# The start of a tuned kernel rearranged: two turns of z in front, casts on another engine, loads in another order

## The chip, the cores and the metric

One core of a Trainium2 chip runs the whole program. The metric is the device time of one execution in microseconds; the median of several executions is quoted. Instruction times come from one profiled execution of each kernel, counted from its first instruction.

## The reference

Eight batches of an attention without softmax, gated by u, then a two-layer network with a sigmoid-approximated GELU over all 24064 tokens:

```python
# u, v: (8, 3008, 256); z: (8, 3008, 64); w_in: (256, 2048); w_out: (2048, 256), all fp32
scores = (1 / S) * matmul(z, z.T)          # S = 3008, per batch
attn   = maximum(scores, 0) ** 2
x      = (u * matmul(attn, v)).reshape(B * S, D)
h      = x @ w_in
out    = (h / (1 + exp(-1.702 * h))) @ w_out
```

## The kernel before

TensorE does everything heavy in fp16. A *scores* step multiplies z by its own transpose into PSUM, ScalarE applies the *relu*, VectorE *squares* it, and TensorE multiplies the square by V (*value matmuls*). For that z must lie transposed in SBUF. In the first batch z is loaded as fp32 in six chunks of up to 512 rows. Each chunk is *cast* to fp16 (two instructions, one for each half of the partitions of the later transpose), *transposed* by TensorE, and *copied* out of PSUM; the three together are called a *turn*. The code counts chunks and turns `g` from 0, this text from 1: turns 3 and 4 are `g` = 2 and 3. V's blocks for the first batch are loaded as fp32 and cast by GpSimd. *Dummy* matmuls on zeros (`keep_warm`) fill idle stretches of TensorE; that they raise its clock or keep it up is what the name intends. TensorE works in the order of the program (before, turns 3 to 6 stand behind 2, 11, 19 and 28 value matmuls, as in the table below), so the tables below decide at which value step a turn, a cast or a scores step stands.

```python
def first_cast(g):                                 # both halves of one chunk's cast, VectorE
    m = g % CB * CB
    for c in range(2):
        dst, src = ZT["st"][g // CB][:, m:m + CB, c, :], ZT["f"][g // CB][:, m:m + CB, :]
        dve.tensor_copy(dst, src)

def first_zt(g):                                   # transposes now, returns the copy for later
    z2 = ZT["st"][g // CB][:, g % CB * CB:(g % CB + 1) * CB]
    if g == 0:
        ...                                        # (cut) turn 1: copied in halves, ScalarE + VectorE
    zp = ZP[g] if g in ZP else ps1.tile([P, CB, P], F16, name="zp", tag="ps1")
    for k in range(CB):
        pe.transpose(zp[:, k, :], z2[:, k, :, :], ident)
    def copies():
        ...                                        # (cut) addresses
        if g > 2:
            act.activation(dst, src, AF.Copy, scale=1.0)
        else:
            dve.tensor_copy(dst, src)
        if nb < CB:
            dve.tensor_copy(zt[:, nb * P:], zp[:, nb, :])
    return copies

def square(b, i, jp, sc):                          # (cut to the first chunk's case)
    rl = pw.tile([P, 2, CH], F16, name="rl", tag="rl", bufs=3)
    act.activation(rl[:, :, :n], sc[:, :, :n], AF.Relu, scale=csc)
    a = pa.tile([P, 2, CH], F16, name="a", tag="a", bufs=26)
    dve.tensor_tensor(a[:, :, :n], rl[:, :, :n], rl[:, :, :n], ALU.mult)

# value step of the first chunk -> turn, cast, number of scores steps
FIRST_ZT, FIRST_CAST = {2: 2, 11: 3, 19: 4, 28: 5}, {2: 3, 8: 4, 16: 5}
SCHED0 = {0: {2: 1, 8: 2, 16: 2, 25: 2, 33: 2, 40: 2}, ...}

# (cut) the start; sp = SyncE's queue, act = ScalarE's
first_z(0, CB, sp)
first_z(CB, 2 * CB, act)
for n0 in (0, VB):
    load_v(0, n0)                # V0: first half on sp, second on act; V1 on sp
first_z(2 * CB, 4 * CB, act)     # z chunks 3 and 4
load_v(0, 2 * VB)
first_z(4 * CB, NJ, sp)          # z chunks 5 and 6
for n0 in range(3 * VB, NJ, VB):
    load_v(0, n0)
keep_warm(7)
for g in range(2):
    first_cast(g)
for copies in [first_zt(g) for g in range(2)]:
    copies()
keep_warm(1)
posts = scores(0, [queue.pop(0) for _ in range(2)])
posts[0]()
first_cast(2)
posts[1]()
keep_warm(3)
posts = scores(0, [queue.pop(0)])
keep_warm(2)
...                          # (cut) PSUM tiles of turns 3 and 4, first load of u
```

The score buffers (`ps2`) are two, the relu buffers three.

Of the kernel before, what the change touches and what calls it, by code (L numbers as in the profile page):

```python
# [15 lines left out]
def kernel(  # L16
# [58 lines left out]
    dve.memset(nil, 0.0)  # L75

    late, LATE = [], []
    ZP = {}
    ZT, V16, UQ, UT, XT, unit, TT = {}, {}, {}, {}, {}, {}, {}

    SYNC = mybir.DependencyInfo(mybir.DependencyClass.Sync, mybir.DependencyReason.DATA)
# [12 lines left out]
    def keep_warm(n):  # L94

        if "w" not in ZT:
            ZT["w"] = ps1.tile([P, CH], F32, name="w", tag="ps1")
        for k in range(n):
            pe.matmul(ZT["w"], nil[:, :P], nil, start=(k == 0), stop=(k == n - 1))  # L99

    def first_z(n0, n1, eng):

        if 0 not in ZT:
            ZT[0] = pz.tile([P, NJ, P], F16, name="ZT", tag="ZT")
            ZT["st"] = [pa.tile([P, CB * CB, 2, DQK], F16, name="zst", tag="tt", bufs=14) for _ in range(2)]
            ZT["f"] = [pw.tile([P, CB * CB, DQK], F32, name="zf", tag="y") for _ in range(2)]
        zf = ZT["f"][n0 // (CB * CB)]
        m0 = n0 % (CB * CB)
        t0, last = n0 * P, n1 == NJ
        t1 = (n1 - CB if last else n1) * P  # L110
        eng.dma_start(
            zf[:, m0:m0 + (t1 - t0) // P, :].rearrange("p (g n) d -> p g (n d)", n=CB),
            z[0, t0:t1].rearrange("(g p n) d -> p g (n d)", p=P, n=CB),
        )
        if last:
            m1 = m0 + (t1 - t0) // P
            eng.dma_start(zf[:, m1:m1 + CB - 1, :], z[0, t1:S0].rearrange("(p n) d -> p n d", n=CB - 1))
            for h in range(2):
                eng.dma_start(zf[h * SREM:(h + 1) * SREM, m1 + CB - 1, :], z[0, S0:S])

    def first_cast(g):
        m = g % CB * CB
        for c in range(2):
            dst, src = ZT["st"][g // CB][:, m:m + CB, c, :], ZT["f"][g // CB][:, m:m + CB, :]
            dve.tensor_copy(dst, src)  # L125

    def first_zt(g):

        z2 = ZT["st"][g // CB][:, g % CB * CB:(g % CB + 1) * CB]
        if g == 0:  # L130
            zh = [ps1.tile([P, CB // 2, P], F16, name="zh", tag="ps1") for _ in range(2)]
            for k in range(CB):
                pe.transpose(zh[k // 2][:, k % 2, :], z2[:, k, :, :], ident)

            def copies():
                dst = ZT[0][:, :CB, :].rearrange("d n p -> d (n p)").rearrange("d (p h n) -> d h p n", h=2, n=CB // 2)
                act.activation(dst[:, 0], zh[0].rearrange("d n p -> d p n"), AF.Copy, scale=1.0)
                dve.tensor_copy(dst[:, 1], zh[1].rearrange("d n p -> d p n"))

            return copies  # L140
        zp = ZP[g] if g in ZP else ps1.tile([P, CB, P], F16, name="zp", tag="ps1")
        for k in range(CB):
            pe.transpose(zp[:, k, :], z2[:, k, :, :], ident)  # L143

        def copies():
            zt = ZT[0][:, g * CB:(g + 1) * CB, :].rearrange("d n p -> d (n p)")
            nb = CB if g < NCH - 1 else CB - 1
            dst = zt[:, :nb * P].rearrange("d (p n) -> d p n", n=nb)
            src = zp[:, :nb, :].rearrange("d n p -> d p n")
            if g > 2:  # L150
                act.activation(dst, src, AF.Copy, scale=1.0)  # L151
            else:
                dve.tensor_copy(dst, src)
# [4 lines that stand above are left out]
# [19 lines left out]
    def load_v(b, n0):  # L177

        if n0 == 0:
            V16[b] = pz.tile([P, NJ, D], F16, name="V16", tag="V16")  # L180
        dst, eng = V16[b][:, n0:n0 + VB], pool
        if b == 0:
            dst, eng = pa.tile([P, VB, D], F32, name="vst", tag="tt", bufs=14), sp
        full = min(VB, NJ - 1 - n0)
        if b == 0 and n0 == 0:
            full = VB // 2
            act.dma_start(dst[:, full:], v[b, full * P:VB * P].rearrange("(n p) c -> p n c", p=P))
        eng.dma_start(dst[:, :full, :], v[b, n0 * P:(n0 + full) * P].rearrange("(n p) c -> p n c", p=P))
        if n0 + VB == NJ:
            for h in range(2):  # L190
                eng.dma_start(dst[h * SREM:(h + 1) * SREM, full, :], v[b, S0:S])
        if b == 0:
            for n in range(0, VB, 2):
                pool.tensor_copy(V16[b][:, n0 + n:n0 + n + 2], dst[:, n:n + 2])
# [380 lines left out]
    def pieces(b, i):  # L575
# [24 lines left out]
    LOADW = {(3, 16): 0, (3, 24): 1, (3, 32): 2, (3, 40): 3, (4, 16): 4, (4, 22): 5, (4, 28): 6, (4, 34): 7}  # L600
    LOAD = {(3, NJ + 20): 4, (4, NJ + 5): 5}

    FIRST_ZT, FIRST_CAST = {2: 2, 11: 3, 19: 4, 28: 5}, {2: 3, 8: 4, 16: 5}
    SCHED0 = {
        0: {2: 1, 8: 2, 16: 2, 25: 2, 33: 2, 40: 2},
        1: {0: 2, 8: 2, 15: 2, 22: 2, 30: 2, 38: 2},
        2: {n: 1 for n in (0, 3, 7, 11, 28, 32, 36, 40, 44)} | {NJ: 2},
        3: {n: 1 for n in (0, 4, 8, 12, 16, 19, 29, 33, 37, 41, 45)} | {NJ: 2},
# [6 lines left out]
    def take(b, n):  # L615
        for post_ in scores(b, [queue.pop(0) for _ in range(n)]):
            post_()
# [7 lines left out]
    first_z(CB, 2 * CB, act)  # L625
    for n0 in (0, VB):
        load_v(0, n0)
    first_z(2 * CB, 4 * CB, act)
    load_v(0, 2 * VB)
    first_z(4 * CB, NJ, sp)  # L630
    for n0 in range(3 * VB, NJ, VB):
        load_v(0, n0)
    keep_warm(7)
    for g in range(2):
        first_cast(g)
    for copies in [first_zt(g) for g in range(2)]:
        copies()
    keep_warm(1)
    posts = scores(0, [queue.pop(0) for _ in range(2)])
    posts[0]()  # L640
    first_cast(2)
    posts[1]()
    keep_warm(3)
    posts = scores(0, [queue.pop(0)])
    keep_warm(2)
    for g in (2, 3):
        ZP[g] = ps1.tile([P, CB, P], F16, name="zp", tag="ps1")
    load_u(0, 1)

    for b in range(B):  # L650
        nup = NCH * NFG
        more = b + 1 < B
        sched = SCHED0 if b == 0 else SCHED if more else SCHED_LAST
        turn, load = (TURN, LOAD) if b else (TURN0, LOAD0)
        head = 0
        for i in range(NCH):
            host = b + 1 if more and i == NCH - 1 else b
            if host > b:
                fill(host)
                LATE.append(host)  # L660
            for n, step in enumerate(attend(b, i, b == 0 and i < 2)):
                if b == 0 and i == 0 and n == 5:
                    load_u(0, 0)
                if b == 0 and i == 0 and n in FIRST_ZT:
                    first_zt(FIRST_ZT[n])()
                if b == 0 and i == 0 and n in FIRST_CAST:
                    first_cast(FIRST_CAST[n])
                if (i, n) in turn:
                    turn_u(b, turn[i, n])
                if (i, n) in load:  # L670
                    load_u(b, load[i, n])
                if b == 0 and (i, n) in LOADW:
                    load_w(LOADW[i, n])
                if more and (i, n) == (NCH - 2, 2):
                    load_z(b + 1)
                if (b, i, n) == (0, NCH - 1, NJ + 4):
                    for sum_ in weight_sums():
                        sum_()
                if (b, i, n) == (0, 0, 2):
                    posts[0]()  # L680
                take(host, sched[i].get(n, 0))
                if i == full(b) and n >= HEAD and (n - HEAD) * LAGY // (2 * NJ - 10) >= head and head < LAGY:
                    up_group(b, head)
                    head += 1
                step()
        late.sort(key=lambda t: t[0])
        if more:
            for i in range(2):
                load_u(b + 1, i)
            for n0 in range(0, NJ, VB):  # L690
                load_v(b + 1, n0)
        prods = products(b)
        for q in range(head, nup):
            if more and q in (head + 14, head + 20):
                k = int(q == head + 20)
                turn_u(b + 1, k)
                load_u(b + 1, k + 2)
            up_group(b, q)
            product(b, *prods.pop(0))
            if q >= 30 and q % 2 and late:  # L700
                late.pop(0)[1]()
        steps = [lambda kp=kp: product(b, *kp) for kp in prods]
        for step in steps:
            step()
            for sum_ in [SUMS.pop(0) for _ in range(min(len(SUMS), 1 + (len(SUMS) > 4)))]:
                sum_()
            for _, turn_it in [late.pop(0) for _ in range(min(len(late), 1 + (len(steps) < 10)))]:
                turn_it()
        LATE.clear()
        if more:  # L710
            while late:
                late.pop(0)[1]()
            take(b + 1, 2)
# [30 lines left out]
```

## Time and profile before

| | before |
|---|---|
| median of 6 executions | 1190.15 us (1189.79 to 1191.45, and one of 3202.51) |
| profiled execution | 1190.33 us, span 1188.2 us |
| TensorE busy | 1181.1 us |
| start of the 114th matmul, of the 118th | 25.94 us, 26.48 us |

The lines on which the reading of this profile rests stand in the prediction. Two things are needed to read them. A timeline line groups neighbouring instructions of one kind; its second column is the time from the start of the first to the end of the last, and the bracket is the idle time just ahead and what ended it. A matmul's printed end is modelled, so two lines of TensorE may overlap (before, the four transposes at 4.15 us end at 4.78, and the next start at 4.58).

One line more is needed as a reference mark. The changed kernel has the same TensorE instructions as this one from the 114th on, so the start of the first value matmul on a transposed square (`o<-tt`), the 118th (the line of scores before it holds four), tells how far all the rest has moved. I call it the *mark*. Before, from the timeline of TensorE:

```profile
25.94 0.61 PE L246 MATMUL sc<-ZT 64*128 64x512 f16 x4
26.48 1.90 PE L360 MATMUL o<-tt,V 128*128 128x512 f16 x8
```

### The profile page before, as it was taken

To read this page: it belongs to the slowest core of one execution; us is meant where nothing else is said; L and a number is where in the kernel's file an instruction comes from. 1 tells how busy PE (TensorE), PEld (TensorE's weight loads), DVE (VectorE), ACT (ScalarE), POOL (GpSimd) and SP (SyncE) were. 2 spreads that over 40 slices of the span, in tenths; PEclk is the share of its full clock that TensorE was granted. 3 is DMA by queue.
4 is the path that set the end of the run, shared out by engine and by line. 5 is a ranking of instruction groups with operands and counts; after the bars stand their busy time and mean duration, and the time that the engine had idled before them with its cause. 6 is when DMAs were issued, how large, how long until landed. Compare 5 with 4: busy or idle time off the path is not lost.

```text
span 1188.2 us, 27887 instructions
## 1 busy us (share of the span) xinstructions
PE 1181.1 (99%) x11529; PEld 724.2 (61%) x11529; DVE 841.9 (71%) x1437; ACT 822.1 (69%) x994; POOL 227.1 (19%) x321
## 2 busy tenths in 40 slices
PE   8999999999999999999999999999999999999998
PEld 3446775467754676547765478554775547855577
DVE  7778765777757786587775878658776587764776
ACT  6877865688646886478864787657876578672785
POOL 4243100331012310133101331014200142001000
PEclk9999999999999999999999999999999999999999
DMA  9998668666688677866879457895568855794012
GB/s 219 167 124 135 125 145 135 87 112 135 134 138 79 112 134 155 130 69 103 156 139 139 68 96 160 152 119 89 103 130 170 105 93 107 140 166 94 1 37 72
DMA packets 374191, 141.82 MB, mean 119 GB/s; under 512 B 315440, under 2 KB 367920, under 8 KB 374064
## 3 DMA queue, kind: packets, MB, share of 16 engines
q1 hardware_dynamic: 316384, 98.87, 46.3%
q0 software_dynamic: 56832, 40.45, 23.1%
q8 instruction: 90, 1.47, 0.5%
q10 hardware_dynamic: 848, 0.72, 0.2%
q14 instruction: 37, 0.30, 0.1%
HBM read 60.29 MB, written 24.64 MB: 71 GB/s over the span
## 4 chain that ended last, share of the span: by engine, by line
PE 98%; DVE 1%; ACT 1%; issue 0%; DVEq 0%; ACTq 0%
PE o L360 39%; PE hg L401 27%; PE st L520 24%; PE sc L246 6%; PE yp L495 1%; ACT rl L262 0%; PE w L99 0%; DVE a L276 0%; DVE zst L125 0%; ACT ZT L151 0%; DVE ut L213 0%; ACT gf L409 0%; DVE WT L448 0%; DVE WT L449 0%; PE zp L143 0%
## 5 line engine op out<-in xcount | busy, mean ns | idle before, releaser
L409 ACT ACTIVATE gf<-hg 128x1024 f32<-128x1024 f32 (+1 forms) x384 | 385.5, 1004 | 139.1 <-PE hg L401 116.4
L262 ACT ACTIVATE rl<-sc 128x1024 f16<-128x1024 f32 (+1 forms) x309 | 294.8, 990 | 160.4 <-PE sc L246 115.0
L360 PEld LDWEIGHTS <-V 64*128 64x128 f16 (+1 forms) x4052 | 239.3, 94 | 234.3 <-issue 12.1
L401 PE MATMUL hg<-xt,W 128*128 128x512 f16 (+1 forms) x1408 | 354.6, 374 | 0.0
L413 DVE TENSOR_SCALAR gt<-gf 128x1024 f16<-128x1024 f32 (+1 forms) x320 | 222.8, 696 | 134.5 <-ACT gf L409 131.9
L360 PE MATMUL o<-a,V 64*128 64x512 f16 (+3 forms) x2286 | 303.2, 368 | 1.7 <-DVE a L276 1.7
L276 DVE TENSOR_TENSOR a<-rl 128x1024 f16<-128x1024 f16 (+1 forms) x274 | 182.7, 670 | 129.0 <-ACT rl L262 128.2
L206 POOL DMA_DIRECT2D uq<-in_u_dram x188 | 128.3, 690 | 696.3 <-PE sc L246 459.6
L360 PE MATMUL o<-tt,V 64*128 64x512 f16 (+1 forms) x1510 | 234.1, 377 | 0.0
L401 PEld LDWEIGHTS <-W 128*128 128x128 f16 x1536 | 139.3, 98 | 119.4 <-issue 2.9
L520 PEld LDWEIGHTS <-gt 128*128 128x128 f16 x2944 | 177.1, 98 | 32.2
L520 PEld LDWEIGHTS <-s 128*128 128x128 f16 x2208 | 133.7, 98 | 25.6 <-issue 0.5
L246 PE MATMUL sc<-ZT 64*128 64x512 f16 (+2 forms) x688 | 119.0, 360 | 0.4
L520 PE MATMUL st<-WT,gt 128*128 128x128 f16 x1472 | 97.8, 219 | 0.0
L520 PE MATMUL st<-WT,s 128*128 128x128 f16 x1472 | 96.5, 219 | 0.2 <-ACT uP L532 0.2
L520 PE MATMUL st<-W,gt 128*128 128x128 f16 x1472 | 96.5, 219 | 0.0
L538 DVE SCALAR_TENSOR_TENSOR y<-st,uP 128x256 f32<-128x256 f32 (+1 forms) x144 | 57.6, 407 | 28.5 <-ACT uP L532 19.9
L532 ACT ACTIVATE uP<-st 128x256 f32<-128x256 f32 (+1 forms) x144 | 53.0, 368 | 31.6 <-DVE y L538 14.7
L377 DVE TENSOR_TENSOR xt<-o,ut 128x512 f16<-128x512 f32 x80 | 51.3, 682 | 23.4 <-PE o L360 23.4
L411 ACT ACTIVATE gt<-gf 128x1024 f16<-128x1024 f32 (+1 forms) x64 | 65.9, 1030 | 2.1
L476 DVE TENSOR_TENSOR s<-s,gt 128x1024 f16<-128x1024 f16 (+1 forms) x96 | 64.9, 676 | 1.1
L474 DVE TENSOR_TENSOR s<-gt 128x1024 f16<-128x1024 f16 (+1 forms) x96 | 64.6, 673 | 0.0
(54 smaller groups left out, 592.4 us busy)
## 6 DMA issues: line engine op xcount, KB each, us to landing
out_dram<-y SPq DMA_DIRECT2D x40, 512.0 KB, 3.5
uq<-in_u_dram POOLq DMA_DIRECT2D x156, 128.0 KB, 3.6
V<-in_v_dram POOLq DMA_DIRECT2D x35, 256.0 KB, 6.4
tt<-a SPq DMA_TRANSPOSE x232, 3.7
uq<-in_u_dram POOLq DMA_DIRECT2D x32, 112.0 KB, 4.7
out_dram<-y SPq DMA_DIRECT2D x7, 384.0 KB, 3.1
vst<-in_v_dram SPq DMA_DIRECT2D x4, 512.0 KB, 6.8
zst<-in_z_dram POOLq DMA_DIRECT2D x7, 192.0 KB, 8.7
```

The lines of the kernel that those rows point to most:

```text
L206: eng.dma_start(uq[k * QW:(k + 1) * QW, :n // QW].rearrange("t q c k -> t q (c k)"), src[:, :, cs])
L246: pe.matmul(sc[:, r, :q1 - q0], zt[h, 2 * kp + r, :], zt[h].rearrange("d n p -> d (n p)")[:, q0:q1], start=True, stop=True,)
L262: act.activation(rl[:, :, :n], sc[:, :, :n], AF.Relu, scale=csc)
L276: dve.tensor_tensor(a[:, :, :n], rl[:, :, :n], rl[:, :, :n], ALU.mult)
L360: ins = pe.matmul(acc[c][:, :n], V16[b][h, j].rearrange("p (c k) -> p k c", k=NCC)[:, c], weights(b, i, j)[h], start=(k, m) == first[c], s ...
L401: pe.matmul(hg[:, e, :n], W1[:, c, ff * P:(ff + 1) * P], XT[b, i][:, c, :n], start=(c == 0), stop=(c == NCC - 1),)
L409: act.activation(gf[:, :, :n], hg[:, :, :n], AF.Gelu_apprx_sigmoid, scale=1.0 / FSC)
L411: act.activation(g, gf[:, :, :n], AF.Copy, scale=FSC)
L413: dve.tensor_scalar(g, gf[:, :, :n], FSC, None, ALU.mult)
L474: dve.tensor_tensor(s_, a21, a22, ALU.add)
L476: dve.tensor_tensor(s_, ST[b, k, "S1", h], a11, ALU.subtract)
L520: pe.matmul(bank[:, m, :], lhs()[:, f, m, :], right[:, ff, :], start=name in ("P1", "P2", "P5") and m == 0 and ff == 0, stop=ff == NFF // ...
```

## The change

Its intent: VectorE makes squares late around 12 and 18 us because casts of z stand ahead of them (two each time, 1.27 and 1.31 us). So chunks 3 and 4 are loaded sooner, cast and transposed before the first value matmul, with dummies between; the casts of chunks 5 and 6 go to ScalarE; the last two turns and some scores steps come some slots sooner, and VectorE copies those turns; V's first two blocks come on ScalarE's queue so that z may have SyncE's.

```diff
-    def first_cast(g):
+    def first_cast(g, by_act=False):
 ...
-            dve.tensor_copy(dst, src)
+            if by_act:
+                act.activation(dst, src, AF.Copy, scale=1.0)
+            else:
+                dve.tensor_copy(dst, src)
 ...                       (first_zt: turn 1's copy in halves removed)
-            if g > 2:
+            if g in (0, 2, 3):
                 act.activation(dst, src, AF.Copy, scale=1.0)
 ...                       (load_v)
-            dst, eng = pa.tile(..., name="vst", ...), sp
+            dst, eng = pa.tile(..., name="vst", ...), act if n0 < 2 * VB else sp
-        if b == 0 and n0 == 0:
-            full = VB // 2
-            act.dma_start(dst[:, full:], v[b, full * P:VB * P]...)
 ...
-    FIRST_ZT, FIRST_CAST = {2: 2, 11: 3, 19: 4, 28: 5}, {2: 3, 8: 4, 16: 5}
+    FIRST_ZT, FIRST_CAST = {12: 4, 20: 5}, {5: 4, 13: 5}
-        0: {2: 1, 8: 2, 16: 2, 25: 2, 33: 2, 40: 2},
+        0: {2: 1, 6: 2, 14: 2, 22: 2, 30: 2, 38: 2},
 ...
-    first_z(2 * CB, 4 * CB, act)
-    load_v(0, 2 * VB)
+    first_z(2 * CB, 4 * CB, sp)
     first_z(4 * CB, NJ, sp)
-    for n0 in range(3 * VB, NJ, VB):
+    for n0 in range(2 * VB, NJ, VB):
 ...
-    keep_warm(1)
     posts = scores(0, [queue.pop(0) for _ in range(2)])
-    posts[0]()
-    first_cast(2)
-    posts[1]()
-    keep_warm(3)
-    posts = scores(0, [queue.pop(0)])
-    keep_warm(2)
+    turns = []
     for g in (2, 3):
-        ZP[g] = ps1.tile([P, CB, P], F16, name="zp", tag="ps1")
+        first_cast(g)
+        keep_warm(2 * g - 2)
+        turns.append(first_zt(g))
+    for post_ in posts:
+        post_()
+    turns[0]()
+    take(0, 1)
 ...                       (in the loop over value steps of the first chunk)
+                if b == 0 and i == 0 and n == 3:
+                    turns[1]()
+                if b == 0 and i == 0 and n in FIRST_CAST:
+                    first_cast(FIRST_CAST[n], True)
```

More of the change, by code (lines that the diff above doesn't have):

```diff
@@ L77 @@
     late, LATE = [], []
-    ZP = {}
     ZT, V16, UQ, UT, XT, unit, TT = {}, {}, {}, {}, {}, {}, {}
@@ L124, in first_cast @@
             dst, src = ZT["st"][g // CB][:, m:m + CB, c, :], ZT["f"][g // CB][:, m:m + CB, :]
-            dve.tensor_copy(dst, src)
+            if by_act:
+                act.activation(dst, src, AF.Copy, scale=1.0)
+            else:
+                dve.tensor_copy(dst, src)
     def first_zt(g):
         z2 = ZT["st"][g // CB][:, g % CB * CB:(g % CB + 1) * CB]
-        if g == 0:
-            zh = [ps1.tile([P, CB // 2, P], F16, name="zh", tag="ps1") for _ in range(2)]
-            for k in range(CB):
-                pe.transpose(zh[k // 2][:, k % 2, :], z2[:, k, :, :], ident)
-            def copies():
-                dst = ZT[0][:, :CB, :].rearrange("d n p -> d (n p)").rearrange("d (p h n) -> d h p n", h=2, n=CB // 2)
-                act.activation(dst[:, 0], zh[0].rearrange("d n p -> d p n"), AF.Copy, scale=1.0)
-                dve.tensor_copy(dst[:, 1], zh[1].rearrange("d n p -> d p n"))
-            return copies
-        zp = ZP[g] if g in ZP else ps1.tile([P, CB, P], F16, name="zp", tag="ps1")
+        zp = ps1.tile([P, CB, P], F16, name="zp", tag="ps1")
         for k in range(CB):
@@ L182, in load_v @@
         if b == 0:
-            dst, eng = pa.tile([P, VB, D], F32, name="vst", tag="tt", bufs=14), sp
+            dst, eng = pa.tile([P, VB, D], F32, name="vst", tag="tt", bufs=14), act if n0 < 2 * VB else sp
         full = min(VB, NJ - 1 - n0)
-        if b == 0 and n0 == 0:
-            full = VB // 2
-            act.dma_start(dst[:, full:], v[b, full * P:VB * P].rearrange("(n p) c -> p n c", p=P))
         eng.dma_start(dst[:, :full, :], v[b, n0 * P:(n0 + full) * P].rearrange("(n p) c -> p n c", p=P))
-        if n0 + VB == NJ:
+        if full < VB:
             for h in range(2):
@@ L663 @@
                     load_u(0, 0)
+                if b == 0 and i == 0 and n == 3:
+                    turns[1]()
+                if b == 0 and i == 0 and n in FIRST_CAST:
+                    first_cast(FIRST_CAST[n], True)
                 if b == 0 and i == 0 and n in FIRST_ZT:
                     first_zt(FIRST_ZT[n])()
-                if b == 0 and i == 0 and n in FIRST_CAST:
-                    first_cast(FIRST_CAST[n])
                 if (i, n) in turn:
@@ L678 @@
                         sum_()
-                if (b, i, n) == (0, 0, 2):
-                    posts[0]()
                 take(host, sched[i].get(n, 0))
```

## The prediction

> **What bounds the kernel now.** I read the busy table first, then the chain that ended last, then TensorE's waits, then the timeline of the first 30 us, which is all that the change touches.
>
> The page's busy table and chain:
>
> ```profile
> PE 1181.1 (99%) x11529; PEld 724.2 (61%) x11529; DVE 841.9 (71%) x1437; ACT 822.1 (69%) x994; POOL 227.1 (19%) x321
> ...
> PE 98%; DVE 1%; ACT 1%; issue 0%; DVEq 0%; ACTq 0%
> ```
>
> TensorE is busy in 99% of a span of 1188.2 us and carries 98% of the chain. A change that leaves TensorE's instructions alone can win only what TensorE is not working on: about 7 us in all, so 2% (23.8 us) is out of reach before any detail is known.
>
> Where those microseconds are shows in the busy time by stretch (columns: stretch, its length, then each engine's busy time and instructions, clock, DMA share, GB/s):
>
> ```profile
> 0.00:12.00 12.00, 10.28 (x45) 3.75 (x46) 6.72 (x15) 6.24 (x7) 4.73 (x12) 1.00 0.89 280
> 12.00:20.00 8.00, 6.80 (x42) 2.88 (x42) 6.75 (x11) 5.66 (x8) 6.98 (x10) 1.00 1.26 216
> 20.00:30.00 10.00, 9.85 (x50) 3.21 (x48) 7.62 (x13) 8.04 (x10) 2.57 (x4) 1.00 1.11 149
> 30.00:40.00 10.00, 10.00 (x52) 3.46 (x50) 7.20 (x11) 8.43 (x9) 2.57 (x4) 1.00 1.06 198
> ```
>
> From 30 us on TensorE is full; between 12 and 20 us it lacks 1.2 us. The timeline says who held it (start, length, engine, line, operation, and in brackets the idle time and what ended it):
>
> ```profile
> 8.26 0.49 DVE L125 CAST zst<-zf 128x256 f16<-128x256 f32 x2 [0.29 <-DMA zf<-in_z_dram]
> ...
> 9.87 1.27 DVE L125 CAST zst<-zf 128x256 f16<-128x256 f32 x2
> ...
> 11.07 1.69 DVE L276 TENSOR_TENSOR a<-rl 128x1024 f16<-128x1024 f16 x2
> ...
> 12.21 0.81 PE L360 MATMUL o<-a,V 128*128 128x512 f16 x3 [0.74 <-DVE a L276]
> ...
> 15.53 1.31 DVE L125 CAST zst<-zf 128x256 f16<-128x256 f32 x2
> ...
> 16.76 1.69 DVE L276 TENSOR_TENSOR a<-rl 128x1024 f16<-128x1024 f16 x2
> ...
> 17.91 0.38 PE L360 MATMUL o<-a,V 128*128 128x512 f16 x1 [0.99 <-DVE a L276]
> ...
> 21.02 0.86 PE L246 MATMUL sc<-ZT 64*128 64x512 f16 x4
> ```
>
> TensorE waits twice, 0.74 and 0.99 us, for a square that VectorE makes late, and each time VectorE had just spent 1.3 us on two z casts put ahead of it. The idle times understate the loss, because a matmul's modelled end runs some 0.16 us past the time at which the next could start. By starts: value matmuls follow one another at 0.216 us, so the one at 12.21 was due at 11.3 and the one at 17.91 at 16.76: 0.9 and 1.15 us lost. The scores at 21.02 were due at about 20.7 and waited for ScalarE's copy of the last turn: 0.3. Together 2.35 us. A further 0.1 us is paid at each of some twelve switches between scores and value matmuls; the change keeps them.
>
> [...] the four casts before 4.3 us take 0.90 us in all with GpSimd idle, a pair takes 1.3 us while GpSimd casts V, and a pair of squares takes 1.69 us there against 1.28 to 1.46 later. So a z cast moved from VectorE to ScalarE saves more than its clean time. [...] The trace has 0.38 us at 256, 0.60 at 512, 0.50 at 384, 1.02 at 1024, so I estimate a z cast on ScalarE at 0.39, a pair at 0.7. [...] The trace's dummies run 0.43 us apart from 1.19 us and 0.22 apart by 8 us.
>
> **The change part by part.** The order of TensorE's instructions in both kernels was compared from the built programs. The same 11529 matmuls are there, dummies too: 7+1+3+2 = 13 before, 7+2+4 = 13 after. From the 114th matmul on (the scores that start at 25.94 us before) both lists agree in shape and order. So the gain is how much sooner that matmul starts.
> - *Loads.* z chunks 3 and 4 (256 KB) were third on ScalarE's queue behind half of V's first block and landed at 8.24. Now they are second on SyncE's, issued at about 1.2, where the first half of V's first block stood, which was 256 KB too and landed at 5.07. I expect 5.0 to 5.5. V's first two blocks go whole on ScalarE's queue: V0 at 6.8 instead of 5.1/5.5, V1 at 9.6 instead of 8.7 (estimates from 330 to 370 GB/s[...]). First use of V0 is about 9, of V1 about 12: both hidden.
> - *Start.* Turn 1 is copied whole by ScalarE, 4.80 to 5.40, instead of in halves by 5.25: first scores at about 5.5 (5.57 before; a dummy is gone from in front of them).
> - *Turns 3 and 4.* VectorE casts both at about 5.9 to 6.8, before GpSimd starts on V and before any square. TensorE: scores to 6.3, two dummies to 7.1, turn, four dummies to 8.3, turn, third scores at about 8.7. That is 1.1 us later than before (7.61), the price of the change: TensorE then has only six value matmuls behind it at the pair of scores that starts at 10.8 (10.87 before, with eight), but turn 4 is already done.
> - *Casts of chunks 5 and 6 on ScalarE.* Four of 0.39: 1.4 us more on ScalarE, which had idle time (2.3 us of 8 between 12 and 20 us). VectorE loses eight casts from between its squares, 0.49+1.27+1.31+1.31 = 4.4 us of the stretch 8 to 17 us (four are made earlier, four go to ScalarE), and turn 3's copy of 0.68; it gets 0.69+0.50+0.21 back in copies of turns 5 and 6, behind squares and not ahead of them.
> - *Walking on* with 1.02 us a relu (0.92 apart), 0.69 to 1.09 a square, 0.216 a matmul: relus of scores 3 and 4 at 9.1 and 10.1; scores 5 and 6 at 10.8 and 11.1; turn 4's copy and a pair of casts 11.0 to 12.2; relus 12.1 and 13.0; scores 7 at 13.5, scores 8 wait 0.3 us for a free score buffer, to 14.05; casts to 14.65; scores 9 and 10 at 16.45 and 16.7 (18.21 and 18.44 before); from there 25 value steps, four scores and the switches, no wait: 11 and 12 at 18.8, 13 and 14 at 21.2, the 114th matmul at 23.6.
>
> Sum: the lost 0.9+1.15+0.3 become 0.1+0.3, and the start gives back up to 0.2 in small differences: 25.94 − 23.6 = 2.3 us, which I round down to **2.2**. After that TensorE is full, and what it uses from DMA lands with slack: the first transposed squares at 17.5 us for a use at 26.5, so nothing pins the later time. (By the page, DMA's busy share stays high to 60 us, but those transfers are released by VectorE and move with it.)
>
> **Rivals.**
> 1. *The casts only move: ScalarE becomes the bound.* For it: from 9.1 to 21.2 us ScalarE has ten relus (9.2 us at 0.92 apart), one copy and four casts (0.5+1.4), 11.1 of 12.1 us; the 0.3 us wait in my walk is of this kind. Against: before, ScalarE idled 1.53 us at 18.65 and 0.81 at 14.69. If each cast pair costs TensorE its 0.7 us, the gain is 1.2: 1188.7.
> 2. *z arrives late, or the clock warms late.* VectorE now has both casts ahead of its first square, in order. If z lands at 8 us as before, everything from the third scores slips about 1.4 us and the gain is 0.9: 1189.0. [...] Against: z has the place that landed at 5.07.
> 3. *Nothing reaches the end.* A later wait on a fixed transfer takes the gain: 1189.9. Against: after 21.1 us the trace has one wait of TensorE over 0.1 us, 0.17 at 103.7, on ScalarE.
> 4. *Better than walked.* If the third scores come by 8.3 and no buffer waits: gain 2.8, 1187.1.
>
> **Range and chances.** The runs of before agree to 0.11 us but for one at 3202.5, which is no property of the kernel; the profiled one took 1190.3. I take 1189.9 − 2.2 = **1187.7**, low 1186.8 (gain 3.1), high 1189.1 (rivals 1 and 2 alone, not both). Faster by 2% would need three times all of TensorE's idle time; slower by 2% would need a fault, or the slow execution that one run showed.
>
> **What would show it.** Right: VectorE's third and fourth cast pairs start before 6.5 us with at most a short wait for z; no wait of TensorE on a square at 12 and 18 us; pairs of scores at about 10.8, 16.5, 18.8 and 21.2; the first matmul on transposed squares about 2.3 us sooner than 26.48; TensorE's busy time less by under 1 us while the span shrinks by about 2.2. Wrong: casts at 8 us (rival 2), dummies 0.43 apart beyond 8 us (the clock), relus back to back with TensorE waiting on them between 11 and 21 us (rival 1), or a span that does not follow the time of that first matmul (rival 3).

The landing times of V0 and V1 (6.8 and 9.6) took the two queues to share the bandwidth evenly, which was the estimate; in the trace of before, the halves of V's first block, 256 KB on each queue behind 128 KB of z, landed 3.9 and 4.3 us after their issue. For a cast pair of 0.7 us on ScalarE the trace of before suffices: 0.38 us for 256 elements, and relus 1.02 us long that start 0.92 apart. That a gap ahead of the first scores could hold the clock back was not shown, so of rival 2 the figures for late z are left. On the transfers that move with VectorE: between 20 and 60 us before, SyncE's transposes waited 19.9 us for squares and GpSimd's loads of u 25.7 us for VectorE's transposes of u.

## The result, and the profile after

| | before | after |
|---|---|---|
| median of 6 executions | 1190.15 us | 1187.82 us (1187.59 to 1188.00, and one of 1193.97) |
| profiled execution | 1190.33 us | 1187.89 us |
| span | 1188.2 us | 1186.0 us |
| idle time of TensorE up to its last matmul, with 1.19 us before the first | 3.53 us | 2.27 us |
| mark | 26.48 us | 24.05 us |

The ratio is 0.9988, with a 95% interval from 0.9965 to 1.001: the same at 2%. (Ratios here are the mean time of one kernel's fast runs over that of the other's of the same rounds, so not quite the ratio of the medians that I quote. The one run of 1193.97 counts in this mean, which is why the interval is wide.)

The page's busy table and chain, after:

```profile
PE 1179.9 (99%) x11529; PEld 723.9 (61%) x11529; DVE 840.9 (71%) x1433; ACT 823.3 (69%) x997; POOL 226.9 (19%) x321
...
PE 98%; ACT 1%; DVE 1%; issue 0%; DVEq 0%; ACTq 0%
```

TensorE still is the bound; its 11529 matmuls are busy for 1.2 us less, and 1.26 us of its idle time are gone. The two do not part the gain into kinds of work: where a value matmul follows another without a wait, its modelled end lies 0.16 us past the start of the next (median up to 40 us, both traces), so fewer waits also mean more overlap. The span is 2.2 us shorter, the last matmul ends 2.45 us sooner (1184.60 and 1182.14 us, rounded), and what follows it is 0.3 us longer in this execution.

The busy time by stretch, after (stretch, its length, busy time and instructions of TensorE, its weight loads, VectorE, ScalarE and GpSimd, clock, DMA share, GB/s):

```profile
0.00:12.00 12.00, 10.35 (x52) 4.10 (x53) 6.18 (x14) 7.64 (x11) 5.50 (x13) 1.00 0.90 284
12.00:20.00 8.00, 7.84 (x47) 3.10 (x45) 6.57 (x10) 7.14 (x10) 7.30 (x10) 1.00 1.26 238
20.00:30.00 10.00, 10.00 (x52) 3.40 (x50) 8.02 (x12) 8.05 (x9) 2.57 (x4) 1.00 1.10 140
```

Between 12 and 20 us TensorE went from 6.80 to 7.84 us busy and starts 5 matmuls more; ScalarE went from 5.66 to 7.14 us. Before 12 us TensorE gains 7 matmuls with only 0.07 us more. The timeline after shows how:

```profile
5.48 0.61 PE L234 MATMUL sc<-ZT 64*128 64x512 f16 x4 [0.26 <-ACT ZT L142]
...
5.86 1.72 DVE L127 CAST zst<-zf 128x256 f16<-128x256 f32 x4
...
6.82 0.40 PE L134 MATMUL zp<-ident,zst 128*128 128x128 f16 x4 [0.20 <-DVE zst L127]
...
8.23 0.39 PE L234 MATMUL sc<-ZT 64*128 64x512 f16 x2
...
8.66 1.94 ACT L250 ACTIVATE rl<-sc 128x1024 f16<-128x1024 f32 x2 [0.33 <-PE sc L234]
...
10.49 0.60 ACT L142 ACTIVATE ZT<-zp 128x512 f16<-128x512 f16 x1
10.96 0.74 ACT L125 ACTIVATE zst<-zf 128x256 f16<-128x256 f32 x2
11.58 1.95 ACT L250 ACTIVATE rl<-sc 128x1024 f16<-128x1024 f32 x2
...
12.65 1.92 DVE L264 TENSOR_TENSOR a<-rl 128x1024 f16<-128x1024 f16 x2 [1.22 <-ACT rl L250]
13.39 0.75 ACT L125 ACTIVATE zst<-zf 128x256 f16<-128x256 f32 x2
13.58 0.39 PE L234 MATMUL sc<-ZT 64*128 64x512 f16 x2 [0.15 <-ACT rl L250]
...
24.05 1.90 PE L348 MATMUL o<-tt,V 128*128 128x512 f16 x8
```

The waits on squares at 12 and 18 us are gone. What is left are four short waits: 0.26 and 0.20 us at the start, 0.15 us for a score buffer at 13.58 (0.32 by starts: TensorE's line before it starts at 13.04, and a scores pair is 0.22 long by issue), and one of 0.17 us at 101 us that was there before too. ScalarE works without a break from 8.66 to 15.97 us, and it is now VectorE that waits, 1.22 us at 12.65. So the pace of this stretch has passed from VectorE to ScalarE, with next to nothing lost on TensorE.

Nothing gives the gain back: matched by number, TensorE's matmuls start 2.43 us sooner at the 114th, between 2.32 and 2.46 sooner from there on, and 2.45 sooner at the last.

### The profile page after: what moved, and what is told of

Its sections match the earlier page's. It is cut to its first block, busy times and chain, and to the rows that moved or that the text cites. A ratio compares the mean times of both kernels' runs of the same rounds, so it can differ in the third digit from the quotient of the medians.

```text
span 1186.0 us, 27884 instructions
## 1 busy us (share of the span) xinstructions
PE 1179.9 (99%) x11529; PEld 723.9 (61%) x11529; DVE 840.9 (71%) x1433; ACT 823.3 (69%) x997; POOL 226.9 (19%) x321
## 4 chain that ended last, share of the span: by engine, by line
PE 98%; ACT 1%; DVE 1%; issue 0%; DVEq 0%; ACTq 0%
PE o L348 40%; PE hg L389 27%; PE st L508 24%; PE sc L234 6%; PE yp L483 1%; ACT rl L250 1%; PE w L98 0%; PE zp L134 0%; DVE a L264 0%; DVE ut L201 0%; ACT gf L397 0%; DVE zst L127 0%; DVE WT L436 0%; DVE WT L437 0%; DVE ZT L144 0%
## 5 line engine op out<-in xcount | busy, mean ns | idle before, releaser
L526 DVE SCALAR_TENSOR_TENSOR y<-st,uP 128x256 f32<-128x256 f32 (+1 forms) x144 | 57.8, 408 | 28.3 <-ACT uP L520 19.9
```

## The experiments

Twelve runs were made, in three calls: ten altered kernels, and the changed one twice more; all gave a correct result. Their diffs are shortened, and a line in words stands for moved loads or a further cut. The kernel before had a median of 1190.19 us in the rounds of the first two calls and 1190.37 in the third. Before they are read, one thing that they brought out has to be known.

**The clock and the mark.** The packed trace records when TensorE's clock goes from half to full speed. (The clock column of the views counts the time before that record as full: it shows 1.00 from the start.) In these fourteen executions that was between 3.83 and 7.21 us after the start, 2.6 to 6.0 us after the first dummy (1.19 us, in e10 1.20), and the spacing of matmuls agrees (a pair of score matmuls at the start is followed by the next after 0.40 us ahead of the record, in e4, and after 0.23 behind it, in e6). The unaltered changed kernel was profiled three times, and its mark moved with the clock: 23.37 us with full clock from 3.83, 24.05 from 5.24, 24.33 from 6.95. (In e5 the transposes of turns 1 and 2 already follow one another at 0.06 us, in the other two at 0.11; in e12 a dummy ahead of turn 3 still takes 0.40.) All of that arises ahead of the third scores, which start at 7.56, 8.23 and 8.52 us; from there to the mark it is 15.81 us in all three traces.

So marks are comparable only at like clock, and for variants of the changed kernel the stretch from the third scores to the mark is the better measure, since the start does not enter it. (For variants of the kernel before it shows only what comes behind their third scores; its turns 3 and 4 lie in that stretch, and in the changed kernel ahead of it.) The last column of this table puts each mark against the changed kernel's at the same clock, by a straight line between those three; for the kernel before the line is drawn on a little. These are estimates, and coarse ones, to some 0.3 us: the trace with 24.05 holds a wait of 0.20 us for a cast that the other two do not have, and the line takes every kernel to shift with the clock as the changed one does, which is not so where a turn waits for z.

| run | median us | ratio to before | full clock from | mark | third scores to mark | mark against the changed kernel at like clock |
|---|---|---|---|---|---|---|
| before | 1190.15 | | 7.21 | 26.48 | 18.87 | +2.1 |
| changed | 1187.82 | 0.9988 | 5.24 | 24.05 | 15.81 | 0 |
| e1_old_loads | 1191.22 | 1.0009 | 6.81 | 26.05 | 15.81 | +1.7 |
| e2_new_loads | 1190.19 | 1.0001 | 4.56 | 25.88 | 19.01 | +2.2 |
| e3_vec_casts | 1188.95 | 0.9991 | 4.54 | 24.95 | 17.15 | +1.2 |
| e4_no_dummies | 1187.90 | 0.9983 | 6.81 | 23.82 | 15.85 | −0.5 |
| e5_after_again | 1188.72 | 0.9999 | 3.83 | 23.37 | 15.81 | 0 |
| e6_before_act_casts | 1188.84 | 0.9988 | 5.29 | 25.37 | 18.40 | +1.3 |
| e7_old_slots | 1187.93 | 0.9981 | 4.44 | 24.07 | 16.31 | +0.4 |
| e8_opt_b | 1187.38 | 0.9979 | 5.48 | 23.45 | 15.48 | −0.6 |
| e9_loads_and_casts | 1188.61 | 0.9982 | 6.25 | 24.76 | 17.46 | +0.5 |
| e10_act_turns | 1187.92 | 0.9977 | 5.83 | 24.15 | 16.14 | 0.0 |
| e11_opt_c | 1187.79 | 0.9975 | 5.20 | 23.58 | 16.21 | −0.5 |
| e12_after_third | 1188.33 | 0.9983 | 6.95 | 24.33 | 15.81 | 0 |

### e1_old_loads: the change with the loads of before

```diff
-  vst on ScalarE's queue for V's first two blocks;  first_z(2 * CB, 4 * CB, sp)
+  vst on SyncE's queue, V0 in halves;               first_z(2 * CB, 4 * CB, act) behind them
```

> The changed kernel with the loads of before: z chunks 3 and 4 third on ScalarE's queue, V on SyncE's. Theory: the early turns stand on the early z. VectorE casts chunks 3 and 4 ahead of its first square, so z landing at about 8.2 us instead of 4.7 moves the third scores from 8.23 to about 10.0 us, ScalarE's chain behind them moves with it, and the first matmul on transposed squares goes from 24.05 to 25.7-25.9 us: 1189.5 us, most of the gain gone. Rival (the order of turns alone does it, the loads are hidden): marker within 0.3 us of 24.05, 1187.9 us.

Measured: mark 26.05, a little later than expected; 1191.22 us (1189.89 to 1192.98). The timelines of VectorE and TensorE:

```profile
5.48 1.03 PE L237 MATMUL sc<-ZT 64*128 64x512 f16 x4 [0.26 <-ACT ZT L142]
...
8.09 1.76 DVE L127 CAST zst<-zf 128x256 f16<-128x256 f32 x4 [2.15 <-DMA zf<-in_z_dram]
8.65 0.40 PE L134 MATMUL zp<-ident,zst 128*128 128x128 f16 x4 [1.43 <-DVE zst L127]
```

The casts wait for z until 8.09 us, TensorE waits 1.43 us for the cast, and of the 2.1 us that the change gains 1.7 are lost. The third scores show it without the line: 10.24 us here, 8.52 in e12, whose clock came at nearly the same time (6.81 and 6.95 us), and from there on the two take the same 15.81 us. With z where it was, putting its turns in front brings the mark 0.4 us forward and gains nothing in the median. The profiled run, 1189.89, fits the mark; the other four lie above 1191, further than the mark explains. They list a mean granted clock of 0.999 to 0.997 where the profiled one lists 1.000. They have no trace, so I don't know where the rest went.

### e2_new_loads: the kernel before with the new loads only

```diff
-  first_z(2 * CB, 4 * CB, act); load_v(0, 2 * VB); first_z(4 * CB, NJ, sp)
+  first_z(2 * CB, 4 * CB, sp); first_z(4 * CB, NJ, sp);   V0 and V1 whole on ScalarE's queue
```

> The kernel before with the loads of the changed one and nothing else. Theory: the loads alone give nothing, because VectorE takes the cast of chunk 3 only after its first square (7.97 us) and the casts stay between the squares: waits of TensorE on a square near 12 and 18 us stay, marker 26.2-26.5 us (26.48 before), 1190.0 us. Rival (z's late landing was the cause of the waits): marker 25.5 or less, 1189.0 us or less.

Measured: 1190.19 us, the same as before; mark 25.88, sooner than the 26.2 to 26.5 expected. The lead is in the start alone: its third scores came at 6.88 us with full clock from 4.56, those of before at 7.61 with full clock from 7.21, and from there to the mark it takes 19.01 us against 18.87. So at like clock the loads alone gain nothing (+2.2 against +2.1). TensorE's waits on squares stayed, now in three places:

```profile
11.21 0.81 PE L357 MATMUL o<-a,V 128*128 128x512 f16 x3 [0.32 <-DVE a L273]
...
14.47 0.81 PE L357 MATMUL o<-a,V 128*128 128x512 f16 x3 [0.61 <-DVE a L273]
...
17.32 0.38 PE L357 MATMUL o<-a,V 128*128 128x512 f16 x1 [0.74 <-DVE a L273]
```

Early z alone is worth nothing here; the loads only make room for the rest.

### e3_vec_casts: the change with the casts of chunks 5 and 6 on VectorE

```diff
-                    first_cast(FIRST_CAST[n], True)
+                    first_cast(FIRST_CAST[n])
```

> The changed kernel with the casts of chunks 5 and 6 on VectorE, at the same slots. Theory of the prediction: taking these casts from between VectorE's squares is what ended the waits, so putting them back costs TensorE 0.5-1.0 us: marker 24.6-25.0, 1188.6 us. Rival, from the trace of the changed kernel: VectorE idles 0.94 us at 9.72 and 1.22 us at 12.65, while ScalarE runs without a break from 8.66 to 15.97 us, so ScalarE is what paces this stretch and the casts fit on VectorE: marker 23.7-24.2, 1187.6 us.

Measured: 1188.95 us (1188.92 to 1189.55), mark 24.95. From the third scores to the mark it takes 17.15 us instead of 15.81, 1.3 us more and a little above the expected size (1.2 at like clock). The form is not as expected:

```profile
12.29 0.40 PE L134 MATMUL zp<-ident,zst 128*128 128x128 f16 x4 [0.27 <-DVE zst L127]
...
16.11 0.40 PE L134 MATMUL zp<-ident,zst 128*128 128x128 f16 x4 [1.05 <-DVE zst L127]
```

TensorE waits for the cast itself, which VectorE makes too late (in the kernel before, a pair took 1.27 to 1.31 us beside GpSimd's casts of V) for a turn that now stands some slots sooner, and not for a square behind it.

### e4_no_dummies: the change without the dummies ahead of turns 3 and 4

```diff
         first_cast(g)
-        keep_warm(2 * g - 2)
         turns.append(first_zt(g))
```

> The changed kernel without the six dummy matmuls around turns 3 and 4. Theory: they only fill a wait. The third scores come at 7.9 instead of 8.23 us (VectorE's last cast ends at 7.57), ScalarE's idle 0.33 us in front of the third relu shrinks, marker 23.7-24.05, 1187.5-1187.8 us. Rival (they hold the clock): matmuls stay 0.43 us apart beyond 8 us, marker 24.5 or later, 1188.3 us or more.

Measured: 1187.90 us (1187.30 to 1188.89), mark 23.82 though its clock rose late, at 6.81. So without dummies the mark came some 0.5 us sooner at like clock; the third scores stand at 7.97 us, against 8.52 in e12. In this trace, with waits of TensorE of 0.32 and 0.42 us for the casts of the two turns, the clock was not lost: the transposes at 6.83 us follow one another at 0.06 us, and 0.11 before. The dummies only fill here, and where one runs at half clock (0.40 us in e12) they push the turn behind them: turn 3 starts at 7.12 us in e12, here at 6.83. Whether other executions lose the clock was not seen; two of the five runs, 1188.89 and 1188.58, list a mean granted clock of 0.998 and have no trace.

### e5_after_again: the change, unaltered, a second time

> The changed kernel unaltered, for the noise of the marker (first matmul on transposed squares, 24.05 us) and of the time beside the other kernels on this chip. The clock record of the six traces so far turns full at 4.5 to 7.2 us, differently in each. If that moves nothing: marker 24.05 within 0.15. If it counts: marker up to 0.5 later when the clock turns full at 7 us. Time 1187.6-1188.2 us.

Measured: 1188.72 us median of 1186.88, 1191.63, 1188.72, 1187.92 and 1192.03. The profiled run, the shortest, has full clock from 3.83 us and its mark at 23.37. That is 0.68 us sooner than in the first profile of the same program: a third of the gain in question. The two long runs have no trace.

### e6_before_act_casts: the kernel before with the casts of chunks 4 to 6 on ScalarE

```diff
-            dve.tensor_copy(dst, src)
+            if g > 2: act.activation(dst, src, AF.Copy, scale=1.0)
+            else:     dve.tensor_copy(dst, src)
```

> The kernel before with one edit: the casts of z chunks 4, 5 and 6 go to ScalarE; loads, turns and slots stay. Theory that casts between the squares are the whole cause: the squares near 12 and 18 us come at once, marker 24.7-25.2, 1188.8 us. Rival, that the later slots and late turns bound it too (the squares' lead is 7 or 8 steps of 0.216 us, less than scores 0.44 + relu 1.02 + square 0.69 us): TensorE still waits on squares, marker 25.4-26.1, 1189.5 us.

Measured: 1188.84 us (1188.48 to 1189.10), mark 25.37, between the two expectations as written. At like clock the casts alone give 2.1 − 1.3 = 0.8 us. No square is waited for any more; what holds TensorE is z and ScalarE's copies:

```profile
9.22 0.40 PE L146 MATMUL zp<-ident,zst 128*128 128x128 f16 x4 [0.89 <-DVE zst L128]
...
14.19 0.61 PE L249 MATMUL sc<-ZT 64*128 64x512 f16 x4 [0.25 <-ACT ZT L154]
```

The cast of chunk 3 started at 7.96 us, behind a wait on the load of z. The wait of 0.89 us is thus of the same kind as in e1. It also makes the 0.8 us too low: a full clock at 7.21 us, as in the kernel before, would bring TensorE later to a turn that waits for z anyway, and shorten this wait but not move the mark (an estimate, from this trace and that of before). Marks as they stand give 26.48 − 25.37 = 1.1 us.

### e7_old_slots: the change with the scores at the slots of before

```diff
-        0: {2: 1, 6: 2, 14: 2, 22: 2, 30: 2, 38: 2},
+        0: {2: 1, 8: 2, 16: 2, 25: 2, 33: 2, 40: 2},
```

> The changed kernel with the score slots of before in the first chunk (8, 16, 25, 33, 40 instead of 6, 14, 22, 30, 38). Theory: the two slots of lead (2 to 3 x 0.216 us for each pair) are needed, as scores, relu and square of one pair take 2.15 us against a lead of 1.5 to 1.7 us; TensorE waits on squares again, 0.3-0.6 us at each of four or five pairs: marker 25.0-25.8, 1189.2 us. Rival (the slots matter little once the casts are gone): marker 24.0-24.4, 1187.9 us.

Measured: 1187.93 us (1187.26 to 1188.90), mark 24.07. My theory, that the sooner slots are worth a microsecond or more, fell: with the old slots TensorE waits 0.12 and 0.23 us for squares, and from the third scores to the mark it takes 0.5 us more (16.31 and 15.81). So the sooner slots are worth half a microsecond. The time does not tell the two apart.

### e8_opt_b: an attempt at a better version

Chunks 5 and 6 are cast by GpSimd between V's second and third block, turn 4 is copied by VectorE behind the second square, and two dummies fewer stand ahead of turn 4.

```diff
-        keep_warm(2 * g - 2)
+        keep_warm(2)
-            if g in (0, 2, 3):
+            if g in (0, 2):
+    for g in (4, 5):
+        first_cast(g, eng=pool)          # behind V0 and V1, ahead of the other blocks of V
```

> A version meant to beat both: the changed kernel with casts of chunks 5 and 6 on GpSimd between its second and third V block, turn 4 copied by VectorE behind its second square, and two dummies fewer in front of turn 4. Theory: ScalarE paces the stretch 8.7 to 16 us; it loses 0.6+0.75+0.75 us of it, the third scores come at 7.9: marker 22.9-23.4, 1186.9 us. Rival: [...] the squares take 1.09 us and V arrives late, marker 24 or later, 1187.8 us or more.

Measured: 1187.38 us, six runs from 1186.86 to 1189.28, ratio 0.9979 with an interval from 0.9967 to 0.9992; mark 23.45, just past the expected 22.9 to 23.4 and 0.6 us ahead of the changed kernel: about half of that lies ahead of the third scores (7.96 and 8.23 us), half behind them (15.48 and 15.81). By stretch, and GpSimd's timeline:

```profile
12.00:20.00 8.00, 8.00 (x47) 3.03 (x45) 7.31 (x10) 6.20 (x7) 8.00 (x10) 1.00 1.19 219
```

```profile
9.76 2.80 POOL L127 CAST zst<-zf 128x256 f16<-128x256 f32 x4
12.51 6.81 POOL L182 CAST V<-vst 128x512 f16<-128x512 f32 x8
```

TensorE is full from 12 to 20 us. GpSimd takes 2.80 us for four casts that take ScalarE 1.49 (0.74 + 0.75), but it had the time. Of all versions this had the lowest median, 0.4 us under the changed kernel; the intervals of the two overlap, so by time alone it is no certain win.

### e9_loads_and_casts: the kernel before with e2's loads and e6's casts

> The kernel before with two parts of the change and not the rest: the loads of the changed kernel, and the casts of chunks 4, 5 and 6 on ScalarE; turns, dummies and score slots stay. The runs so far: loads alone 25.88 (marker), casts alone 25.37, where TensorE waited 0.89 us at 9.22 for a cast that waited for z. If the loads are worth something once the casts are gone, that wait goes: marker 24.3-24.7, 1188.1 us. If the turns in front of the value matmuls are needed, marker stays 24.9 or later, 1188.6 us.

(The edit is those of e2 and e6 together.) Measured: 1188.61 us (1187.89 to 1188.70), mark 24.76, just between the two expectations. The wait of 0.89 us is gone, and one on a copy stays:

```profile
13.58 0.60 PE L246 MATMUL sc<-ZT 64*128 64x512 f16 x4 [0.37 <-ACT ZT L154]
```

So loads that gave nothing alone give 1.3 − 0.5 = 0.8 us once the casts are off VectorE. The turns in front, with the copies and slots, give the last 0.5. This split depends on the clock, as e6's turn waits for z: with full clock at 7.21 us e9's start would be some 0.3 us later (third scores at 7.61, as before, instead of 7.30) and e6's mark the same, so that the loads would give 0.3 us (estimates).

### e10_act_turns: the change with the last two turns copied by ScalarE

```diff
-            if g in (0, 2, 3):
+            if g != 1:
```

> The changed kernel with its last two turns copied by ScalarE as before. Theory: ScalarE has no free time before 16 us, so the copy of turn 5 (0.6 us) moves the relus behind it and TensorE waits 0.4-0.6 us for a score buffer near 16 us; turn 6 falls where ScalarE idles 0.43 us a pair. Marker 0.4-0.6 later than the changed kernel's 23.4-24.05, at the same clock: 23.9-24.6, 1188.3 us. Rival: hidden, marker 23.4-24.1, 1187.9 us.

Measured: 1187.92 us (1187.71 to 1188.29), mark 24.15. One wait for a score buffer is added. TensorE there, first in this run, then in the changed kernel:

```profile
15.74 0.39 PE L234 MATMUL sc<-ZT 64*128 64x512 f16 x2
16.28 0.39 PE L234 MATMUL sc<-ZT 64*128 64x512 f16 x2 [0.15 <-ACT rl L250]
```

```profile
15.96 0.61 PE L234 MATMUL sc<-ZT 64*128 64x512 f16 x4
```

The second pair follows the first after 0.54 us instead of 0.23, so 0.31 us are lost by starts, and from the third scores to the mark it takes 16.14 us instead of 15.81. The wait that the theory named is there, at its place, and a little smaller than the 0.4 to 0.6 us. The column at like clock shows 0.0 because the start of this execution ran 0.2 us ahead (third scores at 8.02 us instead of 8.23: the wait of 0.20 us for a cast is missing here). The time does not tell the two apart. So VectorE's copies of the last two turns are worth about 0.3 us.

### e11_opt_c: e8 with chunk 4 cast by GpSimd as well, and no dummies ahead of turn 4

```diff
-        first_cast(g)
-        keep_warm(2)
+        if g == 2:
+            first_cast(g)
+            keep_warm(2)
+    first_cast(3, eng=pool)              # ahead of V's casts
```

> The version of e8 with chunk 4's cast on GpSimd too, before its first V block, and no dummies in front of turn 4. In the changed kernel VectorE's four casts took 1.72 us instead of 0.9, beside GpSimd's first V casts. Theory: turn 4 is ready by 6.5 us, the first square by 7.3 instead of 8.17, value matmuls start at 7.7: marker 22.7-23.1, 1186.7 us. Rival: ScalarE's relus bound this stretch anyway, marker 23.2-23.5, 1187.3 us.

Measured: 1187.79 us (1186.80 to 1188.12), ratio 0.9975; mark 23.58. The first value matmul stands at 7.82 us, sooner than the 8.29 of e8, but TensorE then waits 0.19 us at 10.22 on a relu and 0.12 at 12.14 on a cast of GpSimd. The third scores start 0.6 us sooner than in e8 (7.37 and 7.96 us), and the stretch behind them is 0.7 us longer (16.21 and 15.48). The mark is no sooner than e8's: starting earlier ran into the next engine.

### e12_after_third: the change, unaltered, a third time

> The changed kernel once more, beside the other three on the same chip. Marker 23.4-24.1, later where the clock record turns full later; time 1187.6-1188.2 us in most runs. Three of its eleven timed runs so far were 4 to 6 us longer, at a recorded clock of 0.998 or 0.999; if that belongs to this kernel, one or two of five will be again.

Measured: 1188.33 us median; the profiled run was the long one, 1190.88 us, and so one long run of the changed kernel has a trace. Its clock is not the cause: full from 6.95 us, the mark is at 24.33. The loss comes later. Its timeline of TensorE:

```profile
5.47 1.03 PE L234 MATMUL sc<-ZT 64*128 64x512 f16 x4 [0.26 <-ACT ZT L142]
...
24.33 1.90 PE L348 MATMUL o<-tt,V 128*128 128x512 f16 x8
...
69.90 1.04 PE L389 MATMUL hg<-xt,W 128*128 128x512 f16 x4 [2.94 <-DMA W<-in_moe_w_in_dram]
```

TensorE waited 2.94 us for the second quarter of the weights w_in. The same tile's answer gives the time from issue to landing, first in this execution, then in the first profile of the same kernel:

```profile
DMA to landing us min/median/max: 11.9/12.4/13.4
```

```profile
DMA to landing us min/median/max: 5.5/8.4/8.8
```

GpSimd issued that quarter at 57.93 and at 57.64 us, so it was not late; it took 11.9 instead of 5.5 us (before: issued at 60.07, 5.3 us). The issue waits for a scores matmul and so moves with TensorE: issue and use both came about 2.4 us sooner, and the slack is about that of before: 66.51 − 63.13 = 3.4 us against 68.94 − 65.33 = 3.6. The change did not shorten it by more than 0.2 us. In this execution the loads of u and the transposes of squares issued from 48 us on also took 1.1 to 7.5 us longer from issue to landing, matched in order. Why transfers were slow then, the trace does not say.

## Why the prediction was right or wrong

**TensorE-bound, 2% out of reach, gain by carry-over: right.** The shift of 2.43 us at the 114th matmul is there at the last one (2.45). TensorE's busy time fell by 1.2 us; under 1 was predicted.

**The loss is VectorE's late squares behind z casts: right.** The waits are gone after the change. Taking only the casts off VectorE (e6) also ended them, and only new loads (e2) did not. The casts ahead were not the whole delay: both squares that TensorE waited for took 1.09 us, while GpSimd cast V, and not 0.69, so some 0.4 us of each wait is the square itself. In e6 and in the changed kernel squares still take up to 1.05 and 1.09 us there, but start sooner.

**The size, 2.2 us: right, partly by two errors that cancel.** The medians differ by 1190.15 − 1187.82 = 2.33 us; in the rounds of e5 and e12 the unaltered kernel gained 1.5 and 2.0 us, so by time the size is known to about a microsecond only, and the mark carries the rest. The prediction's own figures do not quite agree: its waits give 2.35 − 0.4 = 1.95 us and its walk 2.3; 2.2 lies between. One of the waits is read 0.1 us too high, as a value matmul follows the start of two pairs of scores after 0.53 us elsewhere (14.26 to 14.79), so the one at 12.21 was due at 11.40 and not 11.3. The walk said 23.6 us for the 114th matmul, and it started at 23.51. On the way: first scores 5.48 (5.5 predicted); third scores 8.23 (8.7); fifth and sixth 10.39 and 10.65 (10.8 and 11.1); ninth and tenth 15.96 and 16.19 (16.45 and 16.7); 13 and 14 at 20.70 (21.2). So from the third scores on the kernel ran 0.4 to 0.5 us ahead of the walk, and the walk then gave its last group 2.4 us like those before it, with 8 value matmuls, where there are 10 and it took 2.8. The head start comes from the clock for a good part: the walk spaces dummies at half clock up to 7.1 us, as in the trace of before (0.40 us between the first two at 6.54), and here full clock came at 5.24; in e12, where it came at 6.95, the third scores stand at 8.52. That the two cancelled is luck. At like clock the gain is nearer 2.1.

**Loads: right in kind, the times were too cautious.** z chunks 3 and 4 landed at 4.74 us (5.0 to 5.5 predicted), V0 at 5.95 (6.8), V1 at 8.31 (9.6). e1 shows what the step is worth: 1.7 us.

**VectorE's casts at 5.9 to 6.8, before GpSimd starts on V: half wrong.** They started at 5.86 but took 1.72 us, to 7.57, because V0 came sooner and GpSimd cast it from 6.00: the first of the four took 0.28 us, the next two, beside GpSimd's two casts of V (0.61 and 0.67 us, to 7.23), 0.70 each, and the last 0.28; the four of turns 1 and 2, with GpSimd idle, took 0.90 in all. It cost TensorE 0.20 us in this execution and nothing in e5 and e12, since the dummies covered the rest.

**Casts on ScalarE: right.** A pair takes 0.74 and 0.75 us (0.7 predicted); e3 puts the step at 1.3 us.

**The 0.3 us wait of scores 8 for a buffer: right**, 0.32 by starts, at 13.58 instead of 14.05.

**Dummies: the walk gave them no cost beyond the time that they fill.** e4 puts it at about 0.5 us at a late clock: a small gain left lying.

**Rivals.** The first, ScalarE becomes the bound, is seen in form (no break from 8.66 to 15.97 us) but costs TensorE only that 0.32 us. The second, late z, did not happen, and e1 shows that it would have taken most of the gain. The fourth, better than walked (gain 2.8, so a mark of 23.7), came half true: the third scores came by 8.3, but a buffer waits. Its mark was reached by e8 and e11 (23.45 and 23.58), and by the unaltered kernel where the clock came early (23.37 in e5). The third, a later transfer takes the gain, was set aside with "nothing pins the later time". That holds in two of three profiles; in e12 a late weight load took 2.94 us. The prediction looked for such a wait among the transposed squares, and did not name the weights, whose slack is 3 to 5 us in the trace of before.

**What stays open.** Of 16 executions of the changed kernel four took 1190.88, 1191.63, 1192.03 and 1193.97 us, the others 1186.88 to 1188.72. One is explained by the weight load. The other three list a mean granted clock of 0.998, 0.999 and 0.998 and have no trace; shorter runs list 0.999 too, and in e3's trace, listed at 0.999, the only half clock on record lies behind the last matmul. The kernel before has such runs as well (up to 1192.68). Whether the change makes them more frequent can't be said from these.

The shares, by marks at like clock (estimates), are 0.8 us for the casts on ScalarE, then 0.8 for the loads, then 0.5 for turns in front, copies and slots; with what e6 and e9 show of waits for z, about 1 us, 0.3 to 0.9, and 0.4 to 0.7. The medians give 1.35, 0.4 and 0.3 (each against its own rounds of before, the changed kernel as in e12), within noise as large as these steps. So the casts are probably the largest part, and the order of the other two is not shown. They are not separate: loads alone give nothing, and everything but the loads gives 2.1 − 1.7 = 0.4. Taken back singly from the changed kernel, the slots cost 0.5 us and VectorE's copies 0.3.

## What to carry to other kernels

When one engine is 99% busy, list its few waits by starts, find what stood ahead of the late instruction on the engine that it waited for, and move that; here the sum of the waits that went (2.35 − 0.4 us) came within a few tenths of the gain. Such a move often needs a second one (here the loads) that is worth nothing by itself, so test parts both by removal and alone. For gains of a microsecond compare a fixed instruction behind the change, at a like state of the clock, or better the stretch between two instructions behind the start: one execution's start alone shifted the mark by up to 1 us, while that stretch agreed to 0.01 us in three traces.
